# Two 3x3 convolutions by row transforms: in the second layer two of four middle row positions are also nested in columns, the outer weights are streamed per unit, and the output is accumulated in DRAM over x

## The chip, the cores and the metric

The kernel runs on one core of one Trainium2 chip. Times are device microseconds (us) of that core. Each run is marked fast or slow, and only fast runs are compared. With one core in use a run counts as slow when it took over 1.5% longer than the fastest of the same kernel. Where a kernel's own waits vary from run to run, as they will here, this sets aside its worst runs, so that its ratio is somewhat flattered. "PE" is the tensor engine, "PEld" its weight loads, "DVE" the vector engine, "ACT" the scalar engine, "POOL" GpSimd, "SP" the sync engine, which only issues DMA here.

## The reference, cut

```python
def reference(x, t_emb, g1, be1, w1, w_emb, g2, be2, w2):     # x: 2 images, 512 channels, 64 x 64
    h = conv3(silu(gn(x, g1, be1)), w1)                       # 3 x 3 convolution, 512 to 512 channels
    h = h + (silu(t_emb) @ w_emb).reshape(B, C, 1, 1)
    h = conv3(silu(gn(h, g2, be2)), w2)                       # the "second layer"
    return x + h                                              # gn: group norm, 4 groups
```

## The kernel before

Rows are handled in blocks of four output rows by a transform with six row positions (four "middle", two "outer"), so that a block needs fewer products than a direct convolution. In the second layer the outer positions are also transformed in columns ("nested"): 16 column products of 256 columns stand for 24 of them. Each layer has 16 *units* (128 output channels of half an image). Four units share one activation buffer V; they are a *chunk*. There are two V buffers, so the next chunk's V is made during the four units of this one, one input-channel tile after another:

```python
def produce_V(layer, b, ch, ct, nested, due, step, resident=None):
    at, kt = a_ring.next(), k_ring.next()                    # two buffers each
    # ... three DMAs on the sync queue bring h into `at`
    nc.scalar.activation(out=..at.., in_=..at.., func=ACT.Silu, ...)     # 2.3 us
    nc.scalar.activation(out=..kt.., in_=..at.., func=ACT.Copy, scale=4.0)   # 2.0 us
    # ... row transform on DVE, from `at` and `kt` into `kt`
    TT(out=vm(0), in0=Q, in1=S, op=ALU.add)                  # middle row positions into V
    TT(out=vm(2), in0=Q, in1=S, op=ALU.subtract)
    # ...
    TT(out=kt[:, 4 * BLK:6 * BLK], in0=kt[:, 2 * BLK:4 * BLK], in1=kt[:, 0:2 * BLK], op=ALU.subtract)
    kv = lambda o: sub(kt, 4 * BLK + o, [[BLK, 2], [PW, 8], [1, 32]])
    TT(out=nk(2), in0=kv(O), in1=kv(Ee), op=ALU.add)         # column kinds of the outer positions
    TT(out=nk(3), in0=kv(O), in1=kv(Ee), op=ALU.subtract)
    # ... kinds 0 and 1 likewise
```

A unit is a list of steps. Each step accumulates in one of seven PSUM banks, ACT evicts it, DVE combines the evicted parts. `msl`, `nbb` and `nab` are what ACT evicts to:

```python
steps = [("m", s) for s in range(4)] + ([("B", 0), ("B", 1), ("A", 0), ("A", 1)] if nested else ...)
# "m": 4 x 3 matmuls of 512 columns.  "B", "A": 4 x 2 matmuls of 256 columns.
# ...
nc.scalar.activation(out=o, in_=acc[:], func=..., scale=sc)          # evict
# ... at the end of a second-layer unit: DVE adds the outer rows, then
nc.gpsimd.dma_start(out=fq(ys[:]), in_=rows(x), accum_op=ALU.add)    # add x into the unit's output
nc.gpsimd.dma_start(out=rows(out), in_=fq(ys[:]))                    # store it
```

The order of the instructions on every engine is fixed when the kernel is built. A small model walks through all operations, gives each a duration, and appends it to its engine's program at the time at which the model finds it ready. For a DMA the model has a move time by bytes and a fixed lag of 2.6 us until it has landed:

```python
def cost(self, engine, name, args, kw):
    # ...
    if name == "dma_start":
        # ...
        return (0.4 if engine == "sync" else 1.0), 2.6, total / rate
```

Of the kernel before, what the change touches and what calls it, by code (L numbers as in the profile page):

```python
# [10 lines left out]
ACT = mybir.ActivationFunctionType  # L11
# [7 lines left out]

class _Lane:  # L20
# [7 lines left out]
class _Plan:  # L28
# [4 lines left out]
    T0, TU, AHEAD = 35.0, 14.8, 1.0  # L33
# [93 lines left out]
    def order(self):  # L127
# [9 lines left out]
        link, start, fin = 0.0, [0.0] * n, [0.0] * n  # L137
        for i in range(n):
            if self.ops[i][1] == "dma_start" and self.ops[i][3]["in_"].space == DRAM and self.ops[i][4] > -1.0:
                ready[i] = self.T0 + self.TU * (self.ops[i][4] - self.AHEAD)  # L140
            if not left[i]:
                heapq.heappush(pend[self.ops[i][0]], (ready[i], i))
        for _ in range(n):
# [13 lines left out]
            if move:  # L157
                link = done = max(t + busy, link) + move
# [10 lines left out]
    def issue(self, tc):  # L169
        with tc.manual_schedule():  # L170
            for i in self.order():
                engine, name, args, kw = self.ops[i][:4]
                getattr(getattr(self.nc, engine), name)(*args, **kw)  # L173
# [16 lines left out]
def kernel(  # L190
    ctx: ExitStack,
    tc: tile.TileContext,
    x: bass.AP,
    t_emb: bass.AP,
# [3 lines left out]
    w2: bass.AP,  # L198
    out: bass.AP,
# [49 lines left out]
    u1_scr = dpool.tile([CT, P, CT, 2048], F16, name="u1_scr")  # L249
# [200 lines left out]
    def prep_S0(ot, c2, due):  # L450
        um, ur, us = u_slot[ot]
        z = zs.next()
        zv = z[:, 0:12 * P].rearrange("p (c a o) -> p c a o", c=2, a=6)
        plan.at(due - 0.2)
        nc.scalar.activation(out=zv[:, :, 0:4], in_=ur[:, c2:c2 + 2], func=ACT.Copy, scale=WS)
        nc.scalar.activation(out=zv[:, :, 4:6], in_=us[:, c2:c2 + 2, 0].bitcast(BF16), func=ACT.Copy, scale=WS)
        plan.at(due)
        so = us[:, c2:c2 + 2]
        nc.vector.tensor_tensor(out=so[:, :, 1], in0=zv[:, :, 0:4:2], in1=zv[:, :, 1:4:2], op=ALU.add)
        nc.vector.tensor_tensor(out=so[:, :, 0], in0=so[:, :, 1], in1=zv[:, :, 4:6], op=ALU.add)  # L460
        nc.vector.tensor_tensor(out=so[:, :, 1], in0=so[:, :, 1], in1=zv[:, :, 4:6], op=ALU.subtract)
        nc.vector.tensor_scalar(out=so[:, :, :, 0], in0=so[:, :, :, 0], scalar1=0.25, scalar2=None, op0=ALU.mult)

    def prep_U1(ot, ct, due, dve, load):
# [16 lines left out]
        nc.vector.tensor_tensor(out=zf[:, 2:4], in0=zf[:, 0:2], in1=zf[:, 2:4], op=ALU.subtract)  # L481
        plan.at(due + 0.1)
        nc.sync.dma_start(out=u1_scr[ot][:, ct], in_=z[:, 6 * P:ZF])

    def fetch_U1(ot, due):
        plan.at(due)
        um, ur, us = u_slot[ot]
        nc.sync.dma_start(out=um[:].rearrange("p c s n -> p c (s n)"), in_=u1_scr[ot][:, :, 0:1536])
        nc.sync.dma_start(out=us[:].rearrange("p c s g o -> p c (s g o)"), in_=u1_scr[ot][:, :, 1536:2048])
        for ct in range(CT):  # L490
            load_raw(1, ot, ct)
# [24 lines left out]
    def begin_V(layer, b, ch, nested):  # L516
# [3 lines left out]
        if not nested:  # L520
            nc.gpsimd.memset(sub(V, VN, [[VCT, CT], [VW, 33], [1, 2]]), 0.0)

    def produce_V(layer, b, ch, ct, nested, due, step, resident=None):
# [48 lines left out]
        kc = lambda o, st: sub(kt, o * BLK + 1, [[st * BLK, 2], [PW, 16], [1, 32]])  # L572
        Q, S = kc(0, 4), kc(3, 2)
        vm = lambda s: sub(V, ct * VCT + s * VB + 2, [[VB, 2], [VW, 16], [1, 32]])
        TT(out=vm(0), in0=Q, in1=S, op=ALU.add)
        TT(out=vm(2), in0=Q, in1=S, op=ALU.subtract)
        n0 = ct * VCT + VN
        if not nested:
            TT(out=sub(V, n0 + 2, [[VB, 2], [VW, 16], [1, 32]]), in0=kc(2, 1), in1=kc(0, 1), op=ALU.subtract)
            return  # L580
        TT(out=kt[:, 4 * BLK:6 * BLK], in0=kt[:, 2 * BLK:4 * BLK], in1=kt[:, 0:2 * BLK], op=ALU.subtract)

        kv = lambda o: sub(kt, 4 * BLK + o, [[BLK, 2], [PW, 8], [1, 32]])
        nk = lambda k: sub(V, n0 + k * 2 * NH, [[NH, 2], [32, 8], [1, 32]])
        O, Ee = (1, HALF + 1) if layer == 0 else (HALF + 1, 1)
        TT(out=nk(2), in0=kv(O), in1=kv(Ee), op=ALU.add)
        TT(out=nk(3), in0=kv(O), in1=kv(Ee), op=ALU.subtract)
        for k, o in enumerate((0, HALF + 2) if layer == 0 else (2, HALF)):
            TT(out=nk(k), in0=kv(o), in1=kv(k * HALF + 1), op=ALU.subtract)
# [16 lines left out]


    VSLOT = (0, 3, 2, 1)

    NEST = 4  # L610
# [8 lines left out]
    for j, o in enumerate(range(CT)):  # L619
        for c2 in range(0, CT, 2):  # L620
            d = CT * NEST - 1.0 + j + 0.3 * c2
            weight_work.append((CT * NEST - 1.9 + j, lambda o=o, c2=c2, d=d: prep_S0(o, c2, d)))
# [8 lines left out]
    for layer in range(2):  # L631
        for idx, (b, ch) in enumerate(chunks):
            for k, ot in enumerate(range(CT)):
                U = (layer * len(chunks) + idx) * CT + k
                nested = layer == 1 or idx >= NEST
                if k == 0:
                    nxt = (layer,) + chunks[idx + 1] if idx + 1 < len(chunks) else (1,) + chunks[0] if layer == 0 else None
                    if nxt is not None:
                        d0, dc = U - 0.5, 0.85
                        if nxt == (0, 1, 0):  # L640
# [3 lines left out]
                        nest = nxt[0] == 1 or idx + 1 >= NEST  # L644
# [7 lines left out]
                if layer == 1 and idx == 0 and k == 0:  # L652
                    fetch_U1(CT - 1, U)
                um, ur, us = u_slot[ot]
                V = v_buf[(ch + 1) % 2]
# [8 lines left out]
                rows = lambda d, f0=0, f1=8: d[b, ot].rearrange("p (fq t) -> p fq t", fq=8)[  # L664
# [195 lines left out]
```

## Time and profile before

| | us |
|---|---|
| median of the runs (range) | 534.2 (531.99 to 534.33) |
| span of the profiled run | 533.6 |
| end of the first layer in the trace (the prediction worked it back as 300.3) | 299.97 |
| PE busy | 506.3, 95% |
| one second-layer unit | 14.09 |

The lines that show what bounds this layer stand in the prediction. One view that the prediction does not show will matter: how long DMAs took to land between 315 and 450 us. The columns are what was moved, queue, count, KB each, median us from issue to landing.

```profile
out_dram<-z_112 POOLq DMA_DIRECT2D x3, 528.0 KB, 4.6
a_105<-h_scr SPq DMA_DIRECT2D x4, 297.0 KB, 4.2
...
a_104<-h_scr SPq DMA_DIRECT2D x3, 297.0 KB, 4.5
```

An h load is three pieces. The largest (297 KB) landed in 4.2 to 4.5 us, the two smaller ones in 4.3 to 5.4 us, and the stores of a unit's output in 4.6 to 6.0 us (two of the three groups of stores are cut here). "Landing" is counted from issue, so it holds whatever a transfer waits for behind others.

### The profile page before, as it was taken

The page shows a single profiled execution, that of the slowest core. Times are in us where ns is not written, and L with a number is a line of the kernel's source. Part 1 is how long each engine was busy: PE and PEld are TensorE (multiplying, and loading weights), DVE is VectorE, ACT ScalarE, POOL GpSimd, SP SyncE. Part 2 cuts the span into 40 slices and gives each one's busy share as a digit, 9 for nine tenths or more (in the row PEclk, how much of TensorE's full clock was granted, in tenths as well). Part 3 has the DMA queues.
Part 4 walks back from the last instruction along what each step waited for, and adds up shares of the span by engine and source line. Part 5 has one row for each costly group of instructions (what it writes and reads, how often), then busy time and mean ns, then how long its engine had stood idle before and what let it go on. Part 6 is the DMA issues. An engine that isn't in the chain of part 4 may idle for free.

```text
span 533.6 us, 7655 instructions
## 1 busy us (share of the span) xinstructions
PE 506.3 (95%) x2658; PEld 252.0 (47%) x2658; DVE 389.7 (73%) x955; ACT 352.5 (66%) x473; POOL 91.9 (17%) x141
## 2 busy tenths in 40 slices
PE   5796799999999999999999999999999999999994
PEld 3552334444444444444444455555555555555552
DVE  2679999567799996899847887499658963334445
ACT  1869997359689995999669773866466833333332
POOL 3120000002300416000000324111111112111110
PEclk9997899999999999999999999999999999999998
DMA  8537744597488785786799955967777356455564
GB/s 323 168 103 198 213 114 127 145 324 251 126 240 254 213 220 173 214 250 186 203 292 271 288 145 82 163 111 133 123 142 125 51 74 94 70 82 81 82 113 93
DMA packets 108664, 88.85 MB, mean 167 GB/s; under 512 B 8656, under 2 KB 96848, under 8 KB 107600
## 3 DMA queue, kind: packets, MB, share of 16 engines
q1 hardware_dynamic: 74832, 67.79, 42.8%
q0 software_dynamic: 33504, 20.55, 25.7%
q8 instruction: 21, 0.34, 0.3%
q14 instruction: 19, 0.16, 0.1%
q10 hardware_dynamic: 288, 0.01, 0.0%
HBM read 58.32 MB, written 25.69 MB: 157 GB/s over the span
## 4 chain that ended last, share of the span: by engine, by line
PE 86%; DVE 5%; ACT 4%; DMA 2%; issue 1%; POOL 1%; SPq 0%; DVEq 0%; ACTq 0%
PE acc_69 L173 13%; PE acc_66 L173 13%; PE acc_70 L173 12%; PE acc_71 L173 12%; PE acc_67 L173 12%; PE acc_72 L173 12%; PE acc_68 L173 12%; DMA v_108<-in_x_dram 1%; ACT a_104 L173 1%; ACT a_105 L173 1%; DVE msl_77 L173 1%; DVE k_107 L173 1%; DVE k_106 L173 1%; DMA a_105<-in_x_dram 1%; ACT msl_76 L173 1%
## 5 line engine op out<-in xcount | busy, mean ns | idle before, releaser
L173 PEld LDWEIGHTS <-um_81 128*128 128x128 f16 x384 | 37.6, 98 | 55.4 <-issue 7.9
L173 PEld LDWEIGHTS <-um_84 128*128 128x128 f16 x384 | 37.3, 98 | 50.9 <-DVE um_84 L173 3.8
L173 PEld LDWEIGHTS <-um_87 128*128 128x128 f16 x384 | 36.8, 97 | 47.4 <-DVE um_87 L173 1.7
L173 PEld LDWEIGHTS <-um_90 128*128 128x128 f16 x384 | 37.1, 97 | 46.7
L173 DVE TENSOR_TENSOR sts<-msl_77 128x1024 f16<-128x1024 f16 x32 | 20.8, 686 | 44.7 <-ACT msl_77 L173 44.7
L173 DVE TENSOR_TENSOR sts<-msl_76 128x1024 f16<-128x1024 f16 x32 | 20.8, 683 | 35.0 <-ACT msl_76 L173 35.0
L173 POOL DMA_DIRECT2D yst<-nab x16 | 14.6, 915 | 171.8 <-DVE z_111 L173 30.6
L173 ACT ACTIVATE a_104<-a_104,nb_all,sc_all 128x2304 f16<-128x2304 f16 (+1 forms) x14 | 32.3, 2308 | 15.0 <-POOL nb_all L173 11.4
L173 ACT ACTIVATE a_105<-a_105,nb_all,sc_all 128x2304 f16<-128x2304 f16 (+1 forms) x14 | 32.3, 2308 | 0.5 <-DMA a_105<-h_scr 0.5
L173 ACT ACTIVATE k_107<-a_105 128x2112 f16<-128x2112 f16 x16 | 31.5, 1970 | 0.0
L173 ACT ACTIVATE k_106<-a_104 128x2112 f16<-128x2112 f16 x16 | 31.4, 1961 | 0.1
L173 DVE TENSOR_TENSOR z_112<-z_112 128x768 f16<-128x768 f16 (+1 forms) x56 | 24.4, 437 | 0.5
L173 DVE TENSOR_TENSOR z_111<-z_111 128x768 f16<-128x768 f16 (+1 forms) x56 | 24.3, 434 | 0.2
L173 DVE TENSOR_TENSOR k_107<-k_107,a_105 128x1056 f16<-128x1056 f16 x32 | 21.3, 675 | 0.0
L173 DVE TENSOR_TENSOR v_108<-k_106 128x1024 f16<-128x1024 f16 (+1 forms) x36 | 19.9, 579 | 1.8 <-PE acc_71 L173 1.3
L173 DVE TENSOR_TENSOR k_106<-k_106,a_104 128x1056 f16<-128x1056 f16 x32 | 21.1, 677 | 0.0
L173 DVE TENSOR_TENSOR v_108<-k_107 128x1024 f16<-128x1024 f16 (+1 forms) x36 | 20.3, 579 | 0.0
L173 DVE TENSOR_TENSOR v_109<-k_107 128x1024 f16<-128x1024 f16 (+1 forms) x36 | 20.1, 580 | 0.1
L173 DVE TENSOR_TENSOR k_106<-a_104 128x1056 f16<-128x1056 f16 x16 | 11.1, 696 | 12.1 <-ACT a_104 L173 12.1
L173 PE MATMUL acc_70<-v_109,um_81 128*128 128x512 f16 x48 | 12.7, 405 | 7.6 <-DVE v_109 L173 7.6
L173 DVE TENSOR_TENSOR v_109<-k_106 128x1024 f16<-128x1024 f16 (+1 forms) x36 | 19.6, 581 | 0.4 <-DVE z_111 L173 0.3
L173 ACT ACTIVATE msl_77<-yst 128x2112 f16<-128x2112 f16 x8 | 15.7, 1962 | 1.8 <-DMA yst<-nab 1.4
(423 smaller groups left out, 1216.6 us busy)
## 6 DMA issues: line engine op xcount, KB each, us to landing
h_scr<-yst SPq DMA_DIRECT2D x16, 528.0 KB, 5.1
stage_74<-in_w_dram SPq DMA_DIRECT2D x19, 288.0 KB, 3.0
v_108<-in_x_dram SPq DMA_DIRECT2D x4, 1056.0 KB, 7.9
yst<-nab POOLq DMA_DIRECT2D x16, 264.0 KB, 3.7
v_109<-in_x_dram SPq DMA_DIRECT2D x4, 1056.0 KB, 9.3
u_scr<-z_111 SPq DMA_DIRECT2D x8, 512.0 KB, 2.9
u_scr<-z_112 SPq DMA_DIRECT2D x8, 512.0 KB, 3.5
stage_75<-in_w_dram SPq DMA_DIRECT2D x13, 288.0 KB, 3.5
```

The source lines that it names most:

```text
L173: getattr(getattr(self.nc, engine), name)(*args, **kw)
```

## The change

The intent is to take columns from the PE. Two of the four middle row positions of the second layer ("xB" and "xA" below) are nested in columns as the outer ones were, so that two steps of twelve 512-column matmuls become four steps of eight 256-column ones. The larger weights no longer fit on chip beside everything else: the middle ones stay resident, the outer ones are fetched from DRAM for each unit, one unit ahead, into buffers that the first layer used. V holds eight more column products. The output tensor is filled with x during the first layer, and each unit's result is added to it by an accumulating DMA; the separate read of x and the store go. The add of the outer rows moves from DVE to an accumulating DMA as well. The model that orders instructions gets a time per unit for each layer. It also counts the transfers of the GpSimd queue and those of the sync queue on separate links now, so that in the model they no longer delay one another; no run tests this part alone. Core of the diff:

```diff
-    T0, TU, AHEAD = 35.0, 14.8, 1.0
+    T0, TU, AHEAD = 35.0, (15.9, 12.5), 1.0
# ...
+    def stream_U1(n, due):
+        plan.at(due)
+        ot = n % CT
+        sp, ur, us = second_weights(n)
+        nc.sync.dma_start(out=sub(stages.tiles[n % 2], ...), in_=u1_scr[ot][:, :, 0:256])
+        nc.sync.dma_start(out=us[:]..., in_=u1_scr[ot][:, :, 1792:2304])
+        nc.sync.dma_start(out=ur[:]..., in_=w2o[ot])
# ... produce_V, second layer
-        TT(out=kt[:, 4 * BLK:6 * BLK], in0=kt[:, 2 * BLK:4 * BLK], in1=kt[:, 0:2 * BLK], op=ALU.subtract)
-        kv = lambda o: sub(kt, 4 * BLK + o, [[BLK, 2], [PW, 8], [1, 32]])
+        TT(out=sub(at, 0, [[1, 2 * BLK]]), in0=kt[:, 2 * BLK:4 * BLK], in1=kt[:, 0:2 * BLK], op=ALU.subtract)
+        TT(out=sub(at, 2 * BLK, [[BLK, 2], [1, BLK]]), in0=sub(kt, 0, [[4 * BLK, 2], [1, BLK]]),
+           in1=sub(kt, 3 * BLK, [[2 * BLK, 2], [1, BLK]]), op=ALU.add)
+        kv = lambda o: sub(at, o, [[BLK, 4], [PW, 8], [1, 32]])
# ... four column operations of 1024 elements read kv
# ... main loop
+                n = U - 16
+                for j in ((0, 1) if n == -1 else (n + 1,) if 0 <= n < 15 else ()):
+                    stream_U1(j, U + 0.9 + j * (n == -1))
+                if 1 <= U < 16:
+                    fill_out(U - 1, U + 0.5)
# ...
+                    steps = [("xB", 0), ("xB", 1), ("xA", 0), ("xA", 1), ("m", 1), ("m", 2),
+                             ("B", 0), ("B", 1), ("A", 0), ("A", 1)]
# ...
+                    elif kind == "xB":
+                        o, sc, si = nbb[:, s], KAPPA / 2, None
# ...
-                            nc.gpsimd.dma_start(out=fq(ys[:]), in_=rows(x), accum_op=ALU.add)
-                            nc.gpsimd.dma_start(out=rows(out), in_=fq(ys[:]))
+                            nc.gpsimd.dma_start(out=part(out), in_=ys[:], accum_op=ALU.add, ...)
```

Two details that the argument comes back to: the column differences are now written into the `a` buffer (`at`), where the next load but one of h must land; and the iterations n = -1 and n = 0 of the main loop fetch unit 1's outer weights twice (n = -1 fetches units 0 and 1, n = 0 fetches unit 1 again).

> **What bounds the kernel now.** I read the page's busy table and its 40 slices first, then the chain that ended last, then the tensor engine (PE) in order of time inside one unit of the second layer, then the busy times of the other engines by stage, and last the vector engine (DVE) and DMA entry by entry. A "unit" here is 128 output channels of half an image; each layer has 16 units, and four units that share one activation buffer V are called a chunk.
>
> ```profile
> PE 506.3 (95%) x2658; PEld 252.0 (47%) x2658; DVE 389.7 (73%) x955; ACT 352.5 (66%) x473; POOL 91.9 (17%) x141
> PE   5796799999999999999999999999999999999994
> PEclk9997899999999999999999999999999999999998
> PE 86%; DVE 5%; ACT 4%; DMA 2%; issue 1%; POOL 1%; SPq 0%; DVEq 0%; ACTq 0%
> ```
>
> PE is busy in every slice from the seventh to the last but one, at the full granted clock, and 86% of the chain is PE. A busy PE could still be waiting inside, so I checked the spacing. The chain of one second-layer unit, in order of time (start, duration, work):
>
> ```profile
> 441.25 2.65 PE acc_71 L173 x12
> 443.89 2.65 PE acc_72 L173 x12
> 446.54 2.65 PE acc_66 L173 x12
> 449.19 2.65 PE acc_67 L173 x12
> 451.83 0.88 PE acc_68 L173 x8
> 452.71 0.88 PE acc_69 L173 x8
> 453.59 0.87 PE acc_70 L173 x8
> 454.47 0.88 PE acc_71 L173 x8
> 455.34 2.65 PE acc_72 L173 x12
> ```
>
> A step of twelve 512-column matmuls takes 2.648 us (220.7 ns each), a step of eight 256-column ones 0.876 us (109.5 ns each), with no gap between steps. The unit is 441.25 to 455.34 = 14.09 us = 4 x 2.648 + 4 x 0.876. Going back from 511.73, the start of the last unit, in steps of 14.09, the second layer starts at 300.3 and the PE waits for nothing from there to 525.8. So in this layer time is PE columns and nothing else. What the other engines have left, per chunk of four units (four stretches of second layer, the last with three units):
>
> ```profile
> 300.30:356.70 56.40, 56.40 (x323) 31.04 (x321) 43.88 (x103) 36.31 (x46) 17.61 (x27) 1.00 0.74 151
> 356.70:413.10 56.40, 56.40 (x321) 30.97 (x320) 43.24 (x98) 31.98 (x38) 10.24 (x9) 1.00 0.74 129
> 413.10:469.40 56.30, 56.30 (x321) 30.98 (x320) 34.74 (x80) 25.80 (x38) 9.35 (x8) 1.00 0.53 78
> 469.40:511.70 42.30, 42.30 (x242) 23.23 (x240) 16.82 (x37) 14.34 (x24) 6.99 (x6) 1.00 0.53 78
> ```
>
> The columns are the stretch, its length, then busy us of PE, weight load, DVE, ScalarE (ACT) and GpSimd, the granted clock, the DMA share and GB/s. The reader should see that DVE already has 43 us of work in 56 where the next chunk's V is made, and only 5.6 per unit where it is not.
>
> **What the Trainium skill says.** "TensorE: Matmul & The Clock Gate", Back-to-back issue gap, gives N/2.4 + 2.5 ns for one isolated matmul (109.2 ns at 256 columns, 215.8 at 512) and about 131 ns for sustained 512-column ones; this trace shows 109.5 and 220.7, so the isolated formula fits and the sustained figure does not. The same page, LDWEIGHTS, gives 128/1.2 = 107 ns for a weight load whatever the matmul's width; here one takes 97 ns, and the eight-matmul steps hold their 109.5 ns, so a load still hides behind a 256-column matmul, with 12 ns to spare. "VectorE: DVE Perf Modes", The perf-mode tier table, caps a two-tensor operation at two 16-bit elements per cycle; the trace agrees (687 to 704 ns for 1024 elements, 420 for 512), and packed back to back the starts of such operations lie 0.62 and 0.34 us apart. "DMA: Bandwidth & Descriptors", Rules for kernel authors, says an accumulating DMA reads its destination and writes it later with nothing holding the bytes; the change orders the accumulate behind the fill of the output explicitly, so I expect no correctness trouble, and no run shows it yet.
>
> **The change, part by part.**
>
> PE. Before, a second-layer unit has four middle row positions of 12 matmuls of 512 columns and four outer steps of 8 matmuls of 256. Two middle positions stay. The other two become four steps of 16 column products, that is of 8 matmuls of 256 each. New unit: 2 x 2.648 + 8 x 0.876 = 5.30 + 7.01 = 12.30 us. Saved: 14.09 - 12.30 = 1.79 us a unit, 28.7 us over 16 units, all of it on the path that sets the end. The first layer's matmuls stay (72 of 220.7 ns = 15.9 us a unit).
>
> DVE, making V, per input-channel tile: one 1024-element and one 1056-element operation and four of 512 go (0.62 + 0.62 + 4 x 0.35 = 2.64 us), two of 1056 and four of 1024 come (6 x 0.62 = 3.72 us): +1.08 us, or +4.3 us per chunk. DVE, output side, per unit: the add of the two outer rows (0.62) goes to an accumulating DMA, three operations come (2 x 0.34 + 0.62): +0.68 us, +2.7 per chunk. So the 43.2 to 43.9 us of a chunk become about 50.3, while PE needs only 4 x 12.30 = 49.2. DVE and PE are then level in the three chunks that make a V; in the last chunk DVE has some 25 of 49.
>
> ACT: ten evictions of 0.60 us a unit instead of eight, 24 us a chunk, and four V tiles of 2.30 + 1.97 us, 17.1: 41 of 49.2 us.
>
> DMA per second-layer unit: streamed outer weights 256 + 512 + 512 KB = 1.31 MB, at the 300 to 430 GB/s that the DMA timeline shows around 300 us some 3.7 us; the reading of h some 2 us; the accumulate of the outer rows 1.6 us (264 KB, from the software queue's share); the accumulate into the output 528 KB. The old read-and-add of x and store occupied about 4 and 2 us in pieces of 528 bytes; the new one has long rows and I estimate 2 to 3 us. Sum about 10 of 12.3 us. The streamed weights are asked for one unit ahead.
>
> First layer: 15 copies of 528 KB x to the output, about 2 us each. DVE gets three more small operations for each of 16 weight tiles (about 0.2 us each, 10 us) and loses a weight preparation that the second layer never uses (eight groups of four operations, about 1.2 us each, 10 us). They cancel. The V of the first second-layer chunk starts about 0.7 unit later because its buffer is borrowed from weights still in use; it still should end near the seam.
>
> Sum: 534.2 - 28.7 = 505.5 as the floor. Added: DVE excess of 50.3 over 49.2 in three chunks, 3 x 1.1 = 3.3 us; start and seam, about 1 us; the end stays (last middle step, then 11 us of DVE and store), perhaps 0.3 us shorter. Result 509.5 us.
>
> **The rivals.** First, DVE becomes the bound and pulls PE down by more than its excess. For it: the ACT order of the changed kernel puts later evictions ahead of earlier ones that wait for DVE, so the scheduler itself expects DVE to lag; one temporary now serves two pairs of steps in a unit. PE has seven accumulator banks, and with short steps a bank is asked for again after as little as 5.2 us. Against: from 160 to 205 us DVE is 99% busy already and PE does not wait once; the last unit of each chunk has slack in which DVE catches up. If each of 12 units slips to 13.0 us, that adds 8 and gives 516 to 518. Second, streamed weights come late, because the sync queue is in order and a load can stand behind another that waits for DVE: at 13.5 us for 12 units, 520. Against: the order of that queue puts the h loads a chunk ahead of their use, and the DMA sum is 10 of 12.3. Third, the early copies of x collide with the start, where PE already waits for weights (7.6, 2.8 and 1.2 us in the waits) and DMA is at 0.74 to 0.84: 1 to 3 us more, but those waits end with DVE, not with DMA. Fourth, 256-column matmuls without large ones between them run into weight loads of 97 ns: at 120 ns a matmul, 64 x 10 ns x 16 units = 11 us.
>
> **Range and chances.** The floor of 505.5 can be beaten only by something outside the sum, so the low end is 505; one rival in part gives 513, one in full 517, which I take as the high end. Below 523.5 counts as faster by 2%, and two rivals would have to come true together to miss that: 0.95 faster, 0.04 same, 0.01 slower.
>
> **What would show each step right or wrong.** In the last chunk the units should be 12.30 us with steps of 2.65 and 0.88: if not, the PE term is wrong. In the three chunks before, DVE should be near 49 to 51 us busy and PE should show a few short waits whose releaser is ACT or DVE; waits on a streamed-weight tile would speak for the DMA rival. The second layer should take 197 to 202 us instead of 225.5, and the first 300 us should be within 2 us of before. A first layer that is much later, or an end longer than 11 us after the last middle step, would be a cost that I left out.

## The result, and the profile after

The changed kernel is correct. Its four runs had a median of 522.58 us, from 516.11 to 527.63, two of them slow; before it was 534.12 in the same rounds. The ratio of fast runs was 0.9709, with a 95% interval of 0.9633 to 0.9785. (A ratio is the mean time of one kernel's fast runs over that of the other's fast runs of the same rounds, so not quite the ratio of the medians quoted.) It is faster by 2.9%, where 4.6% was forecast (534.2 to 509.5 us), and outside the range of 505 to 517.

The first profile fell in a slow run, so the same kernel was run again unaltered ("after_again" below): 518.1 us, from 516.08 to 523.32, ratio 0.9721 (0.9683 to 0.9758), all fast. (The slow run's trace has more of the waits described below, 16.3 us of PE in the second layer; it is not used.) All lines that follow are from the profiled run of the repeat, a fast one of 518.1 us (its span is 516.4 us). Busy time and PE by slice:

```profile
PE 479.5 (93%) x2786; PEld 265.0 (51%) x2786; DVE 419.1 (81%) x1004; ACT 353.7 (69%) x489; POOL 87.7 (17%) x141
...
PE   5796899999999999999999998998999989999994
```

PE lost 26.8 us of work, and the row of nines of the kernel before now has eights in the second half: PE waits inside the second layer. That layer begins with the first matmul on a streamed tile, at 299.42 here and at 299.97 before, so the first layer cost nothing more:

```profile
299.42 1.04 PE L178 MATMUL acc<-v,stage 128*128 128x256 f16 x8
```

It ends at 508.90 and so lasts 209.5 us, where 197 to 202 were forecast and 225.9 were measured before. Four stretches of 49.2 us, the time that a chunk would take without waits, from 298.5 on (the waits push the real chunks later, by up to 13 us at the end), with the columns of the prediction's windows:

```profile
298.50:347.70 49.20, 46.18 (x322) 31.05 (x321) 43.00 (x92) 36.98 (x51) 18.23 (x26) 1.00 0.97 264
347.70:397.00 49.30, 45.91 (x336) 32.49 (x335) 46.88 (x99) 35.31 (x46) 8.41 (x8) 1.00 0.87 205
397.00:446.10 49.10, 45.02 (x311) 30.05 (x310) 45.47 (x98) 30.89 (x42) 7.25 (x7) 1.00 0.82 187
446.10:495.00 48.90, 48.90 (x351) 33.95 (x350) 27.73 (x60) 24.43 (x44) 9.66 (x9) 1.00 0.78 177
```

Where no V is being made (the last line) PE is busy for 48.90 of 48.90 us, and a unit takes the 12.30 us that were forecast (471.82 to 484.12). In the three stretches that make a V it idles 3.02 + 3.39 + 4.08 = 10.5 us. No engine is full there: DVE has 43 to 47 of 49, ACT 31 to 37. The DMA share has risen from 0.74 and 0.53 to between 0.82 and 0.97. What ended PE's waits from 298 us on (total us, count, longest):

```profile
PE acc L178 <- ACT msl L178: 6.7, 6, 2.4
...
PE acc L178 <- ACT nbb L178: 1.8, 2, 1.2
...
PE acc L178 <- DMA stage<-u_scr: 1.8, 1, 1.8
```

So PE waits mostly for ACT to evict a bank, and once for a streamed-weight tile. Why is ACT late? The chain that ended last, followed back from 450 us, shows a stretch of it in order of time (start, duration, work):

```profile
367.65 5.36 DMA a<-h_scr
373.03 2.32 ACT a L178
375.37 1.96 ACT k L178
377.33 0.98 ACT nbb L178 x2
...
381.99 9.85 PE acc L178 x64
```

and the ACT engine's own instructions at that place (start, duration, work; in brackets what it waited for):

```profile
373.03 2.31 ACT L178 ACTIVATE a<-a,nb_all,sc_all 128x2304 f16<-128x2304 f16 x1 [0.56 <-DMA a<-h_scr]
375.37 1.96 ACT L178 ACTIVATE k<-a 128x2112 f16<-128x2112 f16 x1
377.24 1.07 ACT L178 ACTIVATE nbb<-acc 128x512 f16<-128x512 f32 x2
380.37 1.09 ACT L178 ACTIVATE nbb<-acc 128x512 f16<-128x512 f32 x2 [2.06 <-DVE sts L178]
381.34 1.10 ACT L178 ACTIVATE msl<-acc 128x512 f16<-128x512 f32 x2
```

Read it from the top. An h load issued at 367.65 lands after 5.36 us, and ACT waits for it: next in ACT's program is the activation of that tile. "TensorE: Matmul & The Clock Gate" of the Trainium skill, in "Architectural detail", says that ACT takes its instructions strictly first in, first out, and the trace agrees: the activation (2.3 us) and the copy (2.0 us) go first, then the evictions, two of which wait 2.06 us more because the temporary `nbb` is still being read by DVE. PE had other banks to work on meanwhile: before its next piece, at 381.99, it lost 0.46 us. Its longest wait of this kind, 2.35 us, comes where ACT has both waits one after the other:

```profile
414.69 1.08 ACT L178 ACTIVATE nbb<-acc 128x512 f16<-128x512 f32 x2 [3.96 <-DVE sts L178]
416.95 2.31 ACT L178 ACTIVATE a<-a,nb_all,sc_all 128x2304 f16<-128x2304 f16 x1 [1.17 <-DMA a<-h_scr]
...
422.13 1.15 PE L178 MATMUL acc<-v,um 128*128 128x256 f16 x9 [2.35 <-ACT msl L178]
```

From 298 to 450 us ACT waits 5.5 us for h loads and 24.4 us for DVE to read `nbb`. In the kernel before neither wait occurs between 298 and 470 us. Over the stretch from 298 us to 450 us the loads landed later than before:

```profile
out_dram<-z POOLq DMA_DIRECT2D x6, 528.0 KB, 8.5
a<-h_scr SPq DMA_DIRECT2D x10, 297.0 KB, 5.6
```

From 315 us on, the stretch used for the other kernels, the large piece took 5.7 us.

### The profile page after: what moved, and what is told of

Same layout as the page of the kernel before. It is cut to its first block, busy times and chain, and to the rows that moved or that the text cites. A ratio compares the mean times of both kernels' runs of the same rounds, so it can differ in the third digit from the quotient of the medians.

```text
span 525.9 us, 8064 instructions
## 1 busy us (share of the span) xinstructions
PE 482.6 (92%) x2786; PEld 266.6 (51%) x2786; DVE 419.4 (80%) x1004; ACT 354.0 (67%) x489; POOL 88.1 (17%) x141
## 4 chain that ended last, share of the span: by engine, by line
PE 68%; DMA 13%; ACT 8%; DVE 5%; issue 4%; SPq 1%; POOL 1%; DVEq 0%; ACTq 0%
PE acc_69 L178 11%; PE acc_70 L178 10%; PE acc_66 L178 10%; PE acc_67 L178 10%; PE acc_71 L178 9%; PE acc_72 L178 9%; PE acc_68 L178 9%; DMA a_105<-h_scr 6%; DMA stage_75<-u_scr 3%; DMA a_104<-h_scr 2%; ACT a_105 L178 2%; ACT a_104 L178 1%; SPq L178 1%; ACT k_107 L178 1%; DMA v_108<-in_x_dram 1%
## 5 line engine op out<-in xcount | busy, mean ns | idle before, releaser
L178 POOL DMA_DIRECT2D yst<-nab x21 | 18.8, 895 | 229.0 <-DVE z_111 L178 44.2
L178 ACT ACTIVATE a_104<-a_104,nb_all,sc_all 128x2304 f16<-128x2304 f16 (+1 forms) x14 | 32.3, 2309 | 12.6 <-DMA a_104<-h_scr 6.3
L178 DVE TENSOR_TENSOR z_111<-z_111 128x256 f16<-128x256 f16 (+1 forms) x80 | 31.8, 397 | 0.9
L178 DVE TENSOR_TENSOR z_112<-z_112 128x256 f16<-128x256 f16 (+1 forms) x80 | 31.5, 394 | 1.0
L178 DVE TENSOR_TENSOR sts<-nbb 128x512 f16<-128x512 f16 x64 | 25.9, 422 | 4.9 <-ACT nbb L178 4.5
L178 ACT ACTIVATE msl_76<-yst 128x2112 f16<-128x2112 f16 x8 | 15.7, 1963 | 14.7 <-DMA yst<-nab 14.7
L178 PEld LDWEIGHTS <-ur_88 128*128 128x128 bf16 x192 | 19.6, 103 | 10.0
L178 PEld LDWEIGHTS <-us_89 128*128 128x128 f16 (+1 forms) x160 | 16.1, 100 | 14.1 <-issue 6.2
L178 PEld LDWEIGHTS <-ur_85 128*128 128x128 bf16 x192 | 18.6, 98 | 8.8
L178 ACT ACTIVATE msl_77<-yst 128x2112 f16<-128x2112 f16 x8 | 15.7, 1966 | 8.4 <-DMA yst<-nab 8.4
L178 PEld LDWEIGHTS <-us_86 128*128 128x128 f16 (+1 forms) x160 | 15.5, 97 | 8.0 <-issue 0.6
```

What stands on the lines that cost most here:

```text
L178: inst = getattr(getattr(self.nc, engine), name)(*args, **kw)
```

## The experiments

The theory after this reading: a chain that turns round once per V tile. DVE releases an `a` buffer; the h load is issued, behind weight loads of the same queue; it lands late, because the streams fill the DMA engines; ACT, whose order is fixed, stands on it with evictions queued behind; a bank comes free late; PE waits; DVE gets the evicted parts late. Rivals: (1) DVE alone is too slow, as the prediction's first rival had it; (2) the streamed weights are late and PE waits for them; (3) the order of the sync queue is the cause, and loads asked for earlier, or weight loads moved away, would cure it; (4) the shared temporary `nbb` is. All runs had five rounds against the kernel before, whose medians in them were 532.4 to 534.1. They were made on three chips, so ratios of different batches are compared across chips. And the order of all engines is built anew for each kernel: an edit also moves other instructions. A comparison of the traces finds that of ACT's 489 some 5 (`e_inplace`) to 70 (`e_nodup_nbx`) stand elsewhere than in the kernel that was edited, and more where the order is the change. The one exception is `e_nodup_noout`, which keeps the order of PE, ACT, DVE and the sync queue. In the table a ratio is to the kernel before of the same rounds; "wrong" marks a kernel that does not compute the reference.

| label | what is different from the changed kernel | median us | ratio (95%) |
|---|---|---|---|
| after_again | nothing | 518.10 | 0.9721 (0.9683 to 0.9758) |
| e_nodup | unit 1's weights fetched once | 514.65 | 0.9647 (0.9613 to 0.9680) |
| e_stream_pool | streams issued from GpSimd | 522.68 | 0.9788 (0.9760 to 0.9817) |
| e_nostream | 14 of 16 streams dropped (wrong) | 507.61 | 0.9510 (0.9484 to 0.9536) |
| e_inplace | column differences kept in `k` | 511.62 | 0.9589 (0.9562 to 0.9616) |
| e_nodup_inplace | both | 509.69 | 0.9556 (0.9528 to 0.9585) |
| e_nodup_lite | nodup, 3 DVE operations a unit dropped (wrong) | 508.81 | 0.9527 (0.9493 to 0.9561) |
| e_nodup_nbx | nodup, own temporary for xB | 510.71 | 0.9574 (0.9542 to 0.9605) |
| e_nodup_inplace_nbx | all three | 512.46 | 0.9526 (0.9485 to 0.9566), 3 of 6 slow |
| e_nodup_inplace_early | nodup, in place, h loads asked for 0.8 unit earlier | 510.98 | 0.9570 (0.9539 to 0.9602) |
| e_nodup_noout | nodup, no accumulating store (wrong) | 511.19 | 0.9597 (0.9561 to 0.9633) |
| e_nodup_lag | nodup, ordered for 6.0 us landing of all h loads | 518.24 | 0.9724 (0.9697 to 0.9751) |
| e_nodup_inplace_lag | the same, in place | 521.92 | 0.9774 (0.9746 to 0.9803) |
| e_nodup_inplace_nbx_lag | the same, in place, own temporary | 519.49 | 0.9745 (0.9719 to 0.9771) |
| e_nodup_lag2 | nodup, 6.0 us only for the later three chunks | 512.75 | 0.9621 (0.9597 to 0.9645) |
| e_nodup_inplace_lag2 | the same, in place | 505.85 | 0.9498 (0.9469 to 0.9527) |

Two more (the "nbb2" kernels) were faulty and are told below.

The whole time also holds the first layer, and that varies. Here is the second layer alone, from its first matmul to its last, in the one trace of each kernel (us):

| label | begins | lasts | PE waits in it |
|---|---|---|---|
| kernel before | 299.97 | 225.9 | 0 |
| after_again | 299.42 | 209.5 | 10.3 |
| e_nodup | 295.43 | 208.4 | 8.5 |
| e_nostream | 298.69 | 199.5 | 1.6 |
| e_inplace | 298.34 | 204.7 | 6.3 |
| e_nodup_inplace | 296.12 | 201.9 | 3.8 |
| e_nodup_lite | 297.21 | 202.1 | 3.8 |
| e_nodup_nbx | 300.32 | 201.0 | 3.3 |
| e_nodup_noout | 297.96 | 206.6 | 5.7 |
| e_nodup_lag2 | 299.78 | 203.4 | 3.7 |
| e_nodup_inplace_lag2 | 299.00 | 198.3 | 0.8 |

Without waits it would last 16 x 12.30 = 196.8 us. The beginnings spread by almost 5 us, as much as most of the gains discussed below.

### The streams: repeated, fetched once, from another queue, not at all

The first run repeats the changed kernel.

> The changed kernel unaltered, to learn its spread beside the others. All theories: 514 to 528 us with a profile that has 12 to 23 us of second-layer stalls over 16 units of 12.30 us; if the spread is the stalls themselves, a faster run shows fewer of them and the same unit time in the last chunk.

Unit 1's weights fetched once:

```diff
-                for j in ((0, 1) if n == -1 else (n + 1,) if 0 <= n < 15 else ()):
+                for j in ((0, 1) if n == -1 else (n + 1,) if 1 <= n < 15 else ()):
```

> The outer weights of the second unit of layer two are fetched once instead of twice (the second fetch writes the same data). Duplicate-fetch theory: the 2.6 us wait of PE on the stage tile at the second unit and the half-speed matmuls after it go away, 4 to 6 us less than the changed kernel. If that wait was hidden by later waits anyway (the later chunk ends bind), under 1 us changes.

The three streamed loads from the GpSimd queue, so that h loads no longer stand behind them:

```diff
-        nc.sync.dma_start(...)      # the three of stream_U1
+        nc.gpsimd.dma_start(...)
```

> All streamed outer weights are issued from the GpSimd queue, so that the loads of h no longer stand behind them in the sync queue; same bytes. Queue theory: the 16 us in which ACT waits for the a tile from h falls below 4 us, PE waits on ACT evictions mostly go, total 505 to 512 us. DVE theory: nothing but the first wait changes, still 516 or more, with DVE 99% busy. Traffic theory: landing times of the h loads stay at 6 to 8 us and the waits stay.

And fetches for the first two units alone (later units then multiply by old weights, so the result is wrong on purpose):

```diff
-                for j in ((0, 1) if n == -1 else (n + 1,) if 0 <= n < 15 else ()):
+                for j in ((0, 1) if n == -1 else ()):
```

> Wrong result on purpose: only the first two units' outer weights are fetched, the other fourteen fetches are dropped, so both their traffic and their place in the sync queue are gone. Queue theory and traffic theory: 504 to 509 us, no wait on h. DVE theory: 515 or more, since DVE's work is unchanged. What this gains beyond the GpSimd-queue run is the share of the traffic.

Measured: fetching once gave 0.9647 for 0.9721, some 0.0074 x 533.65 = 3.9 us, more than the single wait of 1.8 us for the stage tile that it took away. The two traces say where the rest may come from: the second layer is only 1.1 us shorter (208.4 for 209.5), but it begins 4.0 us earlier,

```profile
295.43 1.04 PE L178 MATMUL acc<-v,stage 128*128 128x256 f16 x8
```

although ACT, DVE and the sync queue have the same program in both kernels up to 308 us. (The traces part in the first 80 us, where PE waits at the start: the clock granted from 20 to 40 us was 0.91 in one and 0.99 in the other.) So by these traces only about 1 us of the gain is the single fetch's; the rest is not shown to be. Without streams the ratio was 0.9510, 11.3 us better than the changed kernel, and PE idled only 1.7 us in the three chunks (47.79, 49.15 and 48.95 us busy). The landing of the large h piece between 315 and 450 us, and what ACT waited for it, in the kernel without streams:

```profile
a<-h_scr SPq DMA_DIRECT2D x8, 297.0 KB, 3.9
```

```profile
ACT a L178 <- DMA a<-h_scr: 1.2, 3, 0.7
```

So the streams cost nearly all of the loss (this run drops their bytes and their places in the queue together), but not by being late themselves: PE waited for a streamed tile for 1.8 us in all. They delay others. That speaks against rival 2 as the main cause. Moving them to the GpSimd queue made things worse, 0.9788. ACT then waited longer for h than in any other run:

```profile
ACT a L178 <- DMA a<-h_scr: 20.1, 7, 6.4
```

Getting out of one another's queue did not help, then: large h pieces landed in 6.0 us, against 5.7 in the changed kernel. "DMA: Bandwidth & Descriptors", Issuing engines are not separate DMA queues, says that the DMAs of all issuing engines run on the same 16 DMA engines, which fits with that. The run is no clean test of the sync queue, since the GpSimd queue also carries the accumulating DMAs.

### The buffer that a load waits for

In the changed kernel the `a` buffer is read until the last column operation: two operations of 1056 elements that write it and four of 1024 that read it, some 0.70 us each in this trace, so that it is free about 4 us later than when its last reader is the row transform. The edit does the same operations in the same number and sizes, but within `k`:

```diff
-TT(out=sub(at, 0, [[1, 2*BLK]]), in0=kt[:, 2*BLK:4*BLK], in1=kt[:, 0:2*BLK], op=subtract)
-TT(out=sub(at, 2*BLK, [[BLK,2],[1,BLK]]), in0=sub(kt,0,[[4*BLK,2],[1,BLK]]), in1=sub(kt,3*BLK,[[2*BLK,2],[1,BLK]]), op=add)
-kv = lambda o: sub(at, o, [[BLK, 4], [PW, 8], [1, 32]])
+TT(out=sub(kt, 5*BLK, [[-BLK,2],[1,BLK]]), in0=sub(kt, 4*BLK, [[-4*BLK,2],[1,BLK]]), in1=sub(kt, 5*BLK, [[-2*BLK,2],[1,BLK]]), op=add)
+TT(out=kt[:, 2*BLK:4*BLK], in0=kt[:, 2*BLK:4*BLK], in1=kt[:, 0:2*BLK], op=subtract)
+kv = lambda o: sub(kt, 2*BLK + o, [[BLK, 4], [PW, 8], [1, 32]])
```

> On the single-fetch version, the four differences of a V tile are formed inside the k buffer instead of inside the a buffer, with the same number and sizes of DVE operations and the same result; so an a buffer is free for the next load of h before the long column operations, as it was in the kernel before. Buffer-lifetime theory: the wait of ACT for the a tile (9.7 us in the single-fetch profile) falls below 3 us, PE's waits shrink by half or more, 508 to 511 us. Theory that only the traffic of the streamed weights delays the loads: the loads still land 6 us after issue and ACT's wait stays, 514 us.

> The differences formed in the k buffer, with the double fetch of the second unit's weights kept, so that the two causes can be told apart. If they add: about 5 us under the changed kernel's 518, so 512 to 515 us, with the 2 to 3 us wait on the stage tile still there. If the double fetch was the whole trouble and freeing the a buffer only helps behind it: 517 or more.

Measured: 0.9556 for 0.9647 with single fetches (4.9 us), and 0.9589 for 0.9721 with the double one (7.0 us). Both are correct kernels, and neither has less DVE work. What ACT waited for h, first with single fetches alone, then in place as well:

```profile
ACT a L178 <- DMA a<-h_scr: 9.7, 6, 3.3
```

```profile
ACT a L178 <- DMA a<-h_scr: 5.2, 5, 2.7
```

PE's waits for `msl` evictions fell from 7.3 to 3.0 us with it. So the time at which a load's buffer comes free is a link of the chain. Rival 1 in its plain form, DVE as a bound by its amount of work, can't explain a gain at equal work. The double fetch is worth less once this is done: 0.9589 to 0.9556, with overlapping intervals. A third `a` buffer would test the link more directly; it was not run.

### Less DVE work, and a second temporary

Three DVE operations of the output side dropped (the two that combine the xB parts and the one that adds them; wrong on purpose):

```diff
                     if st == ("xB", 1):
-                        TT(out=sv[:, :, 1], in0=b2(0), in1=b2(1), op=ALU.add)
-                        TT(out=sv[:, :, 0], in0=b2(0), in1=b2(1), op=ALU.subtract)
-                    if st == ("xA", 1):
-                        TT(out=mx, in0=mx, in1=sub(sts, 0, [[512, 2], [1, 512]]), op=ALU.add)
+                        pass
```

> Wrong result on purpose: on the single-fetch version, the three DVE operations of each unit that combine the new outer steps are left out, 1.3 us less DVE work a unit, 5.2 us a chunk. DVE theory: 505.5 to 509 us. Load and queue theory: the h loads are released a little earlier but stay late, 511 to 514 us, and PE still waits on ACT for 3 us or more.

Measured: 0.9527, 6.4 us better than with single fetches alone. About 1.3 us of DVE a unit was dropped, 15.6 over 12 units, and it bought 6.4. PE still idled 1.3 + 1.0 + 1.7 = 3.9 us, with DVE at 39 to 44 us of 49. DVE's work is a link too, then, but it is neither the only one nor a full engine.

A temporary of its own for xB was first tried in a region of V that I took to be unused:

```diff
-                        o, sc, si = nbb[:, s], KAPPA / 2, None
+                        o, sc, si = sub(v_buf[1], s * 512, [[1, 512]]), KAPPA / 2, None
# ... and the two DVE operations that read it
```

> On the single-fetch version, the new outer steps are evicted into their own temporary (unused room of an activation buffer) instead of the one that the old outer steps use. Shared-temporary theory: the 30 us in which ACT waits for DVE's reading of that temporary falls by half, PE waits less, 509 to 512 us. If the static order of evictions or the h loads bind instead: 513 to 516 us, and PE's waits on ACT stay near 8 us.

> Both of the two above. If the two waits are separate links of one chain: better than either, 506.5 to 509 us, near the floor of 505.5. If one of them is the whole cause: equal to the better one within 1 us.

Both gave a wrong result, and not on purpose: the region holds column kind 2 of V. The temporary overwrote live data and its accesses added dependencies, so the ratios (0.9565 and, in place, 0.9614) test nothing. The mistake was mine. The repeat puts the temporary in the tails of two other buffers:

```diff
-                        o, sc, si = nbb[:, s], KAPPA / 2, None
+                        o, sc, si = sub(zb[s], YF, [[1, 512]]), KAPPA / 2, None
# ... and the two DVE operations that read it
```

> The separate temporary for the new outer steps again, now in room that really is free (the tail of the two z tiles, 512 columns each): the first try laid it over columns of an activation that PE still reads, so its result was wrong and its time tells nothing. Single fetch. Shared-temporary theory: ACT's wait for DVE's reading of the temporary falls from 30 to under 15 us and the time to 509 to 512 us. Otherwise 513 to 516 us.

> Single fetch, differences in the k buffer, separate temporary. Separate links of one chain: 506.5 to 508.5 us. If the temporary is no cause: 509 to 511 us, as without it.

Both are correct. Alone it gave 0.9574 for 0.9647, 3.9 us; with the in-place edit 0.9526 for 0.9556, with overlapping intervals and half of its runs slow. Rival 4 is a link of the chain as well, and again the gains do not add.

### Order of the queue

h loads of the later three chunks asked for 0.8 unit earlier:

```diff
-        plan.at(due)
+        plan.at(due - (0.8 if layer == 1 and (b, ch) != (0, 0) else 0.0))
```

> Single fetch, differences in the k buffer, and the loads of h asked for 0.8 unit earlier, which puts each of them one group of streamed weights earlier in the sync queue; no other instruction differs in kind. Queue theory (loads stand behind weight loads that wait for PE): ACT's remaining 5 us wait for the a tile goes under 1.5 us, 506.5 to 508.5 us. If the order of the queue does not matter once the buffer is free: 509 to 511 us.

Measured: 0.9570, against 0.9556 without it. No gain. Together with the streams on the GpSimd queue this is a second way of changing what stands ahead of an h load that brought nothing, so nothing supports rival 3 in these two forms. In the changed kernel the sync queue did wait 79.5 us, in 22 waits, for PE to release streamed-weight buffers; a queue that waits is not by that the cause.

### The accumulating store

```diff
-                            nc.gpsimd.dma_start(out=part(out), in_=ys[:], accum_op=ALU.add, ...)
+                            pass
```

> Wrong result on purpose: single fetch, and the accumulating stores into the output are left out (all but the last unit), which takes away 528 KB read, read again and written per unit, but no instruction of PE, DVE or ACT. Traffic theory (the h loads land late because the DMA engines are shared): h lands in 4 to 5 us instead of 6, time 508 to 511 us. If only the queue and the buffers bind: 513 to 516 us.

Measured, wrong on purpose: 0.9597 for 0.9647, 2.7 us, with intervals that overlap a little. Large h pieces landed in 4.2 us, as in the kernel before, and ACT waited 1.2 us for them (9.7 with the stores). Traffic of either kind lengthens the landing. Since PE, ACT, DVE and the sync queue keep their order here, this is the one test of traffic that no new order can explain: after 320 us PE's waits fell from four of 6.1 us in all to one of 2.1 us. Before 320 us, at the seam between the layers, they rose from 2.4 to 3.5 us (the profiled run was the slowest of its six).

### What the fixed order assumes

If the landing is late and ACT's order is fixed for a lag of 2.6 us, then the model could be told the truth: it would put evictions ahead of the activation that has to wait. First for all h loads:

```diff
-            return (0.4 if engine == "sync" else 1.0), 2.6, total / rate
+            far = kw["in_"].space == DRAM and kw["in_"].tensor.name.startswith("h_scr")
+            return (0.4 if engine == "sync" else 1.0), 6.0 if far else 2.6, total / rate
```

> Single fetch; only the scheduler's assumption on when a load of h has landed is changed (6.0 us after its data instead of 2.6; landing is 5.4 to 8 us in the traces), so that the static order of each engine puts more evictions ahead of the activation that waits for the load. No instruction is added or removed. Static-order theory (the order assumes an early landing, so evictions stand behind an activation that waits): PE's waits on ACT fall to 3 us or less and the time to 508 to 511 us. If order matters little: 513 to 516 us.

> The same with the differences formed in the k buffer. Static-order theory: 506 to 508.5 us, spread under 4 us. If the remaining loss is elsewhere (DVE, traffic): 509 to 511 us as without the changed assumption.

> All four: single fetch, differences in the k buffer, separate temporary, later landing assumed. If the three links (buffer, temporary, order) are all of it: at the floor, 504.5 to 507 us, the spread as small as that of the kernel before (2 to 4 us).

All three are correct and slower than without it: 0.9724, 0.9774 and 0.9745. The windows of the first one say why this is not the end of the idea:

```profile
298.50:347.70 49.20, 38.74 (x242) 24.83 (x240) 43.55 (x92) 34.15 (x42) 14.60 (x26) 0.86 0.74 196
347.70:397.00 49.30, 49.17 (x353) 34.05 (x351) 46.84 (x100) 33.57 (x48) 8.62 (x9) 1.00 0.89 211
397.00:446.10 49.10, 49.08 (x352) 33.94 (x350) 46.70 (x102) 37.40 (x49) 8.73 (x9) 1.00 0.91 213
```

The second and third chunk lost 0.15 us in 98.4, with the double use of `a` and the shared temporary still in place. The first chunk lost 10.5 us of waits instead: at the seam between the layers the new order put evictions too late (two waits of PE for an ACT eviction, of 6.1 and 4.2 us, at 305 to 333 us). The matmuls after these two waits also ran slower, at a granted clock of 0.86 over the stretch, which cost some 4 us more (estimate: 12 matmuls of 512 columns took 4.15 us for 2.65 from 311.21 on, and 24 of 256 columns 5.0 us for 2.6 from 333.34 on). The trace shows what stood in front of the eviction that PE waited for:

```profile
308.53 1.96 ACT L179 ACTIVATE msl<-yst 128x2112 f16<-128x2112 f16 x1 [3.97 <-DMA yst<-nab]
...
311.21 4.31 PE L179 MATMUL acc<-v,um 128*128 128x512 f16 x12 [6.11 <-ACT nab L179]
```

It is a statistic over a first-layer output, which waits for the accumulating DMA of the outer rows. In `e_nodup` the last unit's two `nab` evictions stand before that statistic, here behind it. And the large h pieces landed in 4.0 us there (270 to 315 us), less than the 6.0 assumed. ACT waits for this DMA at the seam of the changed kernel as well, 11.0 us in two waits, longer than for h; PE could mostly work on. So the last two kernels keep 2.6 us for the loads up to the seam:

```diff
+            far = ... and self.due > 15
```

> Single fetch, and the later landing (6.0 us) assumed only for the h loads of the three later chunks of layer two, not for the first chunk, where the assumption in the runs before moved the stall to the seam (6 and 4 us waits at 311 and 333 us) while the chunks after it had no PE wait left. Static-order theory: the seam as in the single-fetch run (2 us of waits), later chunks without waits, 506.5 to 509 us, spread under 4 us. If the stall is only moved about by any order: 512 to 516 us.

> The same with the differences formed in the k buffer, meant as the best version. Static-order theory: 505.5 to 508 us, 1 to 3 us under the single-fetch version's like, spread under 4 us. Otherwise 509 to 512 us, as without the changed assumption.

Measured: 0.9621 alone, against 0.9647 without, with overlapping intervals, so that by the whole time it settles nothing alone. (In the traces the second layer is 5.0 us shorter, 203.4 for 208.4, and begins 4.4 us later.) With the in-place edit it gave 0.9498, 505.85 us (503.8 to 508.52), correct. That beats both kernels: 26.5 us under the 532.36 us of before in its rounds, and 12.2 us under the changed one. Its PE by slice, and its first three chunks:

```profile
PE 477.3 (95%) x2786; PEld 264.4 (52%) x2786; DVE 419.9 (83%) x1004; ACT 353.6 (70%) x489; POOL 84.7 (17%) x141
...
PE   4796899999999999999999999999999999999993
```

```profile
298.50:347.70 49.20, 49.20 (x352) 33.95 (x351) 44.77 (x96) 35.22 (x47) 16.63 (x27) 1.00 0.91 240
347.70:397.00 49.30, 48.52 (x345) 33.33 (x343) 48.02 (x102) 37.37 (x51) 8.41 (x8) 1.00 0.93 223
397.00:446.10 49.10, 49.10 (x353) 34.10 (x352) 48.34 (x103) 34.20 (x47) 8.46 (x8) 1.00 0.84 196
```

PE idled 0.8 us in all. The h loads did not land sooner: 6.3 us for the large piece, later than in the changed kernel. ACT still waited 26.4 us from 298 to 450 us for DVE to read `nbb` (24.4 in the changed kernel in the same stretch). But no activation of ACT waits for h any more, by that kernel's list of waits (5.5 us in the changed kernel), and the places in ACT's program have changed: in the changed kernel activation and copy stood side by side at 373.03 and at 402.47, both times right behind a wait for h; here there is always an eviction between them. That pair alone is not the cause, for the kernel without streams has it twice as well and lost little. One place of the new order, in order of time:

```profile
361.72 2.33 ACT L179 ACTIVATE a<-a,nb_all,sc_all 128x2304 f16<-128x2304 f16 x1
363.92 1.10 ACT L179 ACTIVATE nab<-acc 128x512 f16<-128x512 f32 x2
364.87 2.00 ACT L179 ACTIVATE k<-a 128x2112 f16<-128x2112 f16 x1
```

### What is shown, and what stays open

Shown: the loss sits in the three chunks that make a V; without the streams nearly all of it is gone; it also shrinks if the `a` buffer comes free earlier, if `nbb` is not shared, if DVE has less to do or if the accumulating store goes, each alone; and two changes that remove no work, buffer and order, together with the single fetch bring PE to 0.8 us of idle time. Neither of ACT's two waits costs much by itself: without the streams it waited 31.9 us for `nbb` and PE only 1.6 us; with a temporary of its own for xB it waited 11.3 us for h, more than in `e_nodup`, and PE 3.3 us. A loop with no slack fits all of this: shortening any link returns much of the loss, and the gains do not add. On the way to the best kernel the three steps measured (0.9721 - 0.9647) + (0.9647 - 0.9556) + (0.9556 - 0.9498) = 0.0223, or 11.9 us of the 12.6 that were missing; in another order the shares are others, as the double fetch showed, and the first share is mostly not shown to be the fetch's. Open: how much of the loss belongs to the landing and how much to the temporary in the changed kernel itself; how much of each gain, other than that of the dropped stores, comes from the rest of the newly built order; and why the second layer begins up to 5 us earlier in some traces than in others.

## Why the prediction was wrong, point by point

**The PE term was right.** 12.30 us a unit, with steps of 2.65 and 0.88, stand in the last chunk, and the kernel that has almost no waits took 26.5 us less than the kernel before in its rounds, of the 28.7 forecast. Rival four, 256-column matmuls slowed by their weight loads, did not come.

**The step that failed** is the line "Added: DVE excess of 50.3 over 49.2 in three chunks, 3 x 1.1 = 3.3 us; start and seam, about 1 us". What stood over the floor was 518.1 - 505.5 = 12.6 us by the medians (13.1 by the kernel before of the same rounds, 533.65), of which 10.5 us can be seen in the trace as idle PE. The line counted the wrong thing: how full DVE would be. What the runs showed in its place is PE waiting, 8.5 of 10.3 us, for evictions of ACT, which stood in its fixed order behind late h loads and behind a temporary that DVE still read, while every engine had time left.

**The 50.3 itself was wrong, too: too high.** Its increment was right: the second layer's DVE work was 43.88 + 43.24 + 34.74 + 16.82 us before, and 5.6 for the last unit, 144.3 in all; in the best kernel it is 44.77 + 48.02 + 48.34 + 25.80 = 166.9 (the last term is from that kernel's fourth chunk), 22.6 more, against 3 x 7.0 + 2.7 = 23.7 forecast. But it was added to the two fullest of three chunks. Added to their mean of 40.6 it gives 47.6, and 47.0 was measured. By the prediction's own criterion there was no excess at all.

**DMA: the share was about right and the use of it was not.** "Sum about 10 of 12.3 us" is 0.81; 0.82 to 0.97 were measured. The prediction took from it that there was room. It never asked what a nearly full set of DMA engines does to the landing of an h load: 4.2 us before, 5.6 after, 3.9 without the streams. Rival two looked for the danger in weights that stand behind others in the queue. It was the reverse: the weights came in time but for 1.8 us, and h was late.

**Rival one named the size, and part of the evidence.** "516 to 518" is what came in the fast runs (518.1), by luck as far as the size goes, and the prediction quoted both links, evictions placed in a fixed order and a shared temporary. It set them aside because DVE had been 99% busy between 160 and 205 us without a PE wait. That stretch is in the first layer, with 15.9 us a unit and no streams, and says nothing of a layer with 12.3. The range ended at 517 although the prediction had itself priced rival one at up to 518 and rival two at 520. Rival one's mechanism, DVE as the bound, was not what happened: equal DVE work ran without stalls.

**The rest held.** The first layer was within 2 us (299.4 against 300.0), so the copies of x and the weight work were hidden and rival three did not come. (The prediction's argument that PE's early waits end with DVE had left out one of 5.9 us for the load of x; it did no harm.) ACT came out at 31 to 37 us a stretch, not 41. The end, from the last middle step on, was 11.0 us, against 11.3 before. The PE waits did have ACT as their releaser, as the prediction's list of signs had it, and a wait for a streamed tile did show.

## What to carry to other kernels

When a change takes time out of the bounding engine, don't only compare each other engine's busy time with the new total; follow one turn of every buffer (released, load issued, landed, processed, bank freed), with landing times as they will be under the new traffic, and ask whether the turn still fits. Where the order on an in-order engine is fixed at build time, the latencies it was built with are part of the kernel: after adding traffic, measure landings again and rebuild the order, for the stage where they changed alone. If shortening any of several links brings back most of a loss, it is a loop without slack, and gains measured one by one must not be added. When a gain is a few us, compare the stage that the edit touches and not the whole time alone: here that stage began up to 5 us earlier or later from trace to trace.

## What the Trainium skill lacked or had wrong

- "DMA: Bandwidth & Descriptors", Anatomy of one DMA, gives a DMA of the GpSimd path as 2.0 us and bytes at 436 GB/s, which makes 3.2 us (an estimate from that page) of a 528 KB transfer. It does not say what accumulating into DRAM costs: here such a DMA landed in 8.1 to 8.5 us from issue, in the best kernel in 9.2 to 9.9, while the plain store before took 4.6 to 6.0 (medians).
- The same page says that the fixed cost of a DMA grows with the load on the memory, but has no figure for a load's landing under mixed traffic. Here a 297 KB load on the sync queue landed in 3.9 us without the streamed weights, 4.2 to 4.5 in the kernel before, 5.6 with them and 6.3 in the best kernel.
- "TensorE: Matmul & The Clock Gate", Back-to-back issue gap, states about 131 ns for sustained 512-column matmuls. Here they are 220.7 ns apart over whole layers; the same section's formula for an isolated one, 215.8 ns, is the nearer.
- No page warns that a static order on an in-order engine carries assumed latencies. Assuming 6.0 us in place of 2.6 for h loads after the seam, with the in-place edit, took the ratio from 0.9556 to 0.9498; assuming it everywhere took it to 0.9774.
